# Windowed attention and two feed-forward stages on one core: a fixed step for the attention halves, and new addresses for the split operands

## The chip, the cores and the metric

The kernel runs on one core of one Trainium2 chip. The time is device microseconds (us) of one execution, the median of three runs. The profile is of one further execution, taken by the hardware profiler.

## What is computed

Queries, keys and values of 4 batches, 8 heads, 576 positions and width 64 go through attention in which a position sees itself and the 63 before it. The result, 2304 tokens by 512, passes two feed-forward stages:

```python
scores = scale * np.matmul(q, k.transpose(0, 1, 3, 2))
mask = (rel >= 0) & (rel < window)            # window = 64
attn = softmax(np.where(mask, scores, -1e9))
x = np.matmul(attn, v)                        # then 2304 x 512
a = x @ w1                                    # 512 x 1024
b = x @ w2
x = (a * b @ w3) @ w_out                      # 1024 x 1024, 1024 x 512
h = x @ w_in                                  # 512 x 2048
out = (h * sigmoid(h)) @ w_out2               # 2048 x 512
```

## The kernel before

**Stages.** Weights first (0 to 88.9 us of the trace): they come as 64-bit floats, are unpacked on ScalarE, VectorE and GpSimd, and `w3 @ w_out` is formed on TensorE. Then phase A, nine blocks (`blk` 0 to 8) of 256 tokens: per block 192 products on line 718 (tiles `ab`: a and b, 16 steps `s` of 12 products) and 96 on line 743 (tile `x`). Then the stage for `h` (line 1028) and the output stage (line 1179), from 476.8 us to the end.

**Products.** Every operand is kept as a rounded ("high") part and the rest ("low"), both fp32r. One product of matrices is three passes (`PASSES`): high by high, high weight by low data, low weight by high data. The data are the moving operand, 256 columns in phase A and in the output stage. `split` makes the parts: a CAST on ScalarE (line 117) for the high one, a subtraction on GpSimd or VectorE (line 120) for the low one. The tiles are `xa`, `xb` (tokens into phase A) and `p` (a times b); within a tile the high part began 544 and 2096 elements of 4 bytes into it, the low part 0 and 16. 544 elements are 2176 bytes, 8 x 256 + 128; 2080 are 8320, 32 x 256 + 128: the two parts began 128 bytes apart within a stretch of 256. In the output stage all high and low moving operands begin at one offset within 256 bytes.

**Attention.** 74 groups `g` of two heads and a window of queries; 14 run in the weight stage, 60 within phase A. A group has two halves. `half(2g)` (even) issues on TensorE the scores of group g (tile `s`, lines 399 to 407), the values of group g-2 (tile `o`, lines 483, 484) and the transposes of group g-1 (tile `t`, line 450); on VectorE it issues the row maximum (line 414) and the splits of the transposes (lines 463, 465), on ScalarE their CASTs (460, 462) and the exponentials (line 428). `half(2g+1)` (odd) has the normalisation on VectorE (lines 436, 438, 440), which the transposes of the next even half wait for, the sum of the values (491 to 495), and the splits and loads of a later group. Some groups (`plain`) come split already and have fewer steps. All engines run their instructions in the order of the program.

**What sets the order.** `unit(n)` stands ahead of every 12 products (24 units a block). It calls `halves_to`, which runs halves up to number 28 + (24 blk + n + 1) * 5 // 7: 5 halves in 7 units. Halves thus stand 12 or 24 products apart, even ones mostly 36 and sometimes 24. Attention ends with block 6; blocks 7 and 8 have products alone.

**`w_in`.** 16 pieces of `w_in` are converted during phase A: a load on SyncE's queue (line 149, into `xe`), `scale` and `rest` on ScalarE (224, 229), `fraction`, `sign(0)`, `sign(1)` on VectorE (232, 236) with an addition on GpSimd (241) behind the last, and a store (244). `between` holds these steps by unit; `squeeze` runs those that are due in a unit, in an even half and after an evacuation. Loads and stores hang on `moves`.

**Blocks 7 and 8.** The operands of the next stage (`x_raw`, `x_sum`, `x_op`; loads of line 988) are made by `hooks_x` in block 7 from its unit 0 on, and parts of `w_in` are loaded (`r_load`, line 852) in unit 19 of block 7 and unit 0 of block 8.

## Time and profile before

| | us |
|---|---|
| Median of three runs | 827.35 (826.8 to 829.11) |
| Profiled execution, its own time | 829.54 |
| Its span in the trace | 827.8 |
| TensorE busy | 806.9 (97%) |
| VectorE, ScalarE, GpSimd busy | 633.0, 554.1, 339.4 |
| Weight stage | 88.9 |
| Phase A, blocks 0 to 6 | 320.0 |
| Phase A, blocks 7 and 8 | 67.9 |
| Stage for `h` and output stage | 351.0 |

The profile gives for each engine the time in which one of its instructions ran, and for each idle stretch what ended it. A matmul is busy from its start to its end, and the next one starts before that end: a busy TensorE can still run at different spacings. "Mean ns" of a matmul is the length of one, not the spacing.

### The profile page before, as it was taken

To read this page: it belongs to the slowest core of one execution; us is meant where nothing else is said; L and a number is where in the kernel's file an instruction comes from. 1 tells how busy PE (TensorE), PEld (TensorE's weight loads), DVE (VectorE), ACT (ScalarE), POOL (GpSimd) and SP (SyncE) were. 2 spreads that over 40 slices of the span, in tenths; PEclk is the share of its full clock that TensorE was granted. 3 is DMA by queue.
4 is the path that set the end of the run, shared out by engine and by line. 5 is a ranking of instruction groups with operands and counts; after the bars stand their busy time and mean duration, and the time that the engine had idled before them with its cause. 6 is when DMAs were issued, how large, how long until landed. Compare 5 with 4: busy or idle time off the path is not lost.

```text
span 827.8 us, 17223 instructions
## 1 busy us (share of the span) xinstructions
PE 806.9 (97%) x5930; PEld 762.2 (92%) x5930; DVE 633.0 (76%) x1537; ACT 554.1 (67%) x1278; POOL 339.4 (41%) x404
## 2 busy tenths in 40 slices
PE   8999999999998999999999999999999999999998
PEld 3455799899998999999999999999999999999998
DVE  7888858888888887898561669765654899998782
ACT  6899768888888887888541567765656664443340
POOL 5678656676866776777422402444100000000000
PEclk9999999999999999999999999999999999999999
DMA  9998243444543555454313128999567755554421
GB/s 309 336 315 284 74 157 101 135 150 151 176 151 114 159 164 166 135 160 128 115 52 102 64 97 301 314 300 371 206 245 251 238 165 157 165 156 131 151 77 51
DMA packets 81526, 146.44 MB, mean 177 GB/s; under 512 B 7072, under 2 KB 47904, under 8 KB 81440
## 3 DMA queue, kind: packets, MB, share of 16 engines
q1 hardware_dynamic: 76384, 140.47, 51.9%
q10 hardware_dynamic: 5056, 4.88, 1.8%
q8 instruction: 47, 0.77, 0.4%
q14 instruction: 39, 0.32, 0.1%
HBM read 105.48 MB, written 39.85 MB: 176 GB/s over the span
## 4 chain that ended last, share of the span: by engine, by line
PE 60%; ACT 10%; DVE 9%; issue 6%; POOL 3%; DMA 2%; SPq 0%; ACTq 0%; DVEq 0%; POOLq 0%
PE ab L718 12%; PE oa L1179 10%; PE ob L1179 8%; PE x L743 7%; PE ha L1028 6%; PE hd L1028 6%; PE hb L1028 6%; PE hc L1028 3%; ACT sm L428 2%; DVE a L726 1%; POOL klo L373 1%; ACT qkhi L367 1%; DVE sm L414 1%; PE t L450 1%; DVE sm L440 1%
## 5 line engine op out<-in xcount | busy, mean ns | idle before, releaser
L718 PE MATMUL ab<-xa,hl 128*128 128x256 f32 x864 | 128.2, 284 | 0.1
L718 PE MATMUL ab<-xb,hl 128*128 128x256 f32 x864 | 125.2, 280 | 0.0
L718 PEld LDWEIGHTS ab<-xa,hl 128*128 128x128 f32 x864 | 111.4, 188 | 0.9 <-DVE wp L120 0.9
L718 PEld LDWEIGHTS ab<-xb,hl 128*128 128x128 f32 x864 | 111.9, 188 | 0.0
L743 PE MATMUL x<-p,wp 128*128 128x256 f32 x864 | 109.1, 285 | 0.0
L743 PEld LDWEIGHTS x<-p,wp 128*128 128x128 f32 x864 | 105.0, 191 | 0.0
L1179 PE MATMUL oa<-wo_w,hi 128*128 128x256 f32 x408 | 73.7, 276 | 0.0
L373 POOL TENSOR_TENSOR klo<-qk,qkhi 64x192 fp32r<-64x192 f32 x110 | 70.6, 642 | 7.2 <-ACT qkhi L367 3.1
L120 POOL TENSOR_TENSOR p<-a,p 128x512 fp32r<-128x512 f32 x36 | 48.7, 1354 | 47.5 <-ACT p L117 47.5
L1179 PEld LDWEIGHTS oa<-wo_w,hi 128*128 128x128 f32 x408 | 61.4, 188 | 0.0
L1179 PE MATMUL oa<-wo_w,lo 128*128 128x256 f32 x204 | 56.3, 276 | 0.0
L117 ACT CAST p<-a 128x512 fp32r<-128x512 f32 x36 | 22.4, 621 | 49.0 <-DVE a L726 49.0
L1028 PE MATMUL ha<-xop,wi_w 128*128 128x384 f32 x288 | 53.9, 336 | 0.0
L428 ACT ACTIVATE sm<-sm,nm 128x192 f32<-128x192 f32 x110 | 49.3, 449 | 5.5 <-DVE nm L414 3.9
L1028 PEld LDWEIGHTS ha<-xop,wi_w 128*128 128x128 f32 x288 | 50.1, 188 | 0.1
L495 POOL TENSOR_TENSOR xr<-ot 128x128 f32<-128x128 f32 x43 | 25.4, 590 | 55.1 <-DVE ot L494 42.5
L1028 PE MATMUL hd<-xop,wi_w 128*128 128x384 f32 x252 | 47.6, 336 | 0.0
L414 DVE CUSTOM_DVE_ANT_0 sm<-s,consts 128x192 f32<-128x192 f32 x144 | 45.5, 353 | 2.3 <-PE s L407 1.1
L726 DVE TENSOR_TENSOR a<-ab,a 128x512 f32<-128x512 f32 x36 | 24.9, 691 | 29.2 <-PE ab L718 28.5
L367 ACT CAST qkhi<-qk 128x768 fp32r<-128x768 f32 x55 | 45.9, 834 | 1.2
L896 POOL TENSOR_TENSOR cv_b<-cv_b,cv_r 128x512 int32<-128x512 int32 x16 | 22.8, 1422 | 58.3 <-ACT wi_w L880 28.4
L450 PE MATMUL t<-consts,sm 128*128 128x128 f32 x216 | 35.9, 275 | 10.6 <-DVE sm L440 6.8
(276 smaller groups left out, 2190.9 us busy)
## 6 DMA issues: line engine op xcount, KB each, us to landing
qk<-in_qkv SPq DMA_DIRECT2D x55, 384.0 KB, 3.1
gd<-gxa SPq DMA_DIRECT2D x24, 384.0 KB, 5.0
words<-in_w SPq DMA_DIRECT2D x16, 512.0 KB, 6.6
xe<-in_w_in SPq DMA_DIRECT2D x16, 512.0 KB, 5.1
gq<-in_w_out SPq DMA_DIRECT2D x16, 512.0 KB, 5.6
words<-in_w3t SPq DMA_DIRECT2D x15, 512.0 KB, 6.7
gd<-gst SPq DMA_DIRECT2D x18, 384.0 KB, 5.1
xe<-gd SPq DMA_DIRECT2D x13, 512.0 KB, 4.1
```

The source lines that it names most:

```text
L120: (nc.vector if eng_lo == "dve" else nc.gpsimd).tensor_tensor(out=lo, in0=src, in1=f32(hi), op=ALU.subtract)
L367: nc.scalar.copy(out=hi, in_=t)
L373: nc.gpsimd.tensor_tensor(out=k_lo[g % 2][hs, h * 192 : h * 192 + 192], in0=t[hs, n], in1=f32(hi[hs, n]), op=ALU.subtract)
L414: nc.vector.tensor_tensor_reduce(out=sm[g % 2][:, h, :], in0=s_ps[:, h, :], in1=consts[:, at + 64 - 64 * h : at + 256 - 64 * h], op0=ALU.a ...
L428: nc.scalar.activation(out=e[:, h, :], in_=x, func=AF.Exp, scale=-1.0, bias=nm[:, h : h + 1], accum_out=sums_of[g % 2][:, h, 0:1])
L450: nc.tensor.transpose(t_ps[:, i * 128 : i * 128 + 128], x[:, at : at + 128], id_sb)
L495: nc.gpsimd.tensor_tensor(out=to, in0=t[:, 0:128], in1=t[:, 128:256], op=ALU.add)
L718: nc.tensor.matmul(acc[:, j * NA : j * NA + NA], lhsT=w[:, l, fs], rhs=x[k // 2][r][:, k % 2], start=(j == 0 and k == 0 and n == 0), stop= ...
L726: nc.vector.tensor_tensor(out=a_sb[:, 1], in0=acc, in1=a_sb[:, 0], op=ALU.mult)
L743: nc.tensor.matmul(acc[:, o * NA : o * NA + NA], lhsT=wp[f][:, l, at : at + 128], rhs=p[r][:, f], start=(n == 0), stop=((o, f) not in [y[: ...
L1028: nc.tensor.matmul(bank[name][:, q, 0:NB], lhsT=w[:, l, first + kt], rhs=x[:, kt, r, :], start=(fresh and kt == 0 and n == 0), stop=(kt == ...
L1179: nc.tensor.matmul(dst, lhsT=lhs[l], rhs=rhs[r], start=(first and e == 0 and q == 0 and n == 0), stop=(e == DUOS - 1 and q == 1 and n == 2 ...
```

## The change

Four things change; no instruction is added or removed on any engine. **(1)** In `xa` and `xb` the parts now begin at elements 32 and 544, in `p` at 48 and 2096: 2048 bytes (8 x 256) and 8192 bytes (32 x 256) apart, one offset within 256 bytes. **(2)** `tick`, ahead of every product, runs a half every 18 products, so that an even half stands every 36, at the same eight places in each block (products 6, 42, ... 258); the last half falls at product 132 of block 7. **(3)** The passes of `w_in` are keyed by the even half (`between`, one pass on VectorE in each of three groups in a row) and by the product (`moves`: load 104 products ahead, `scale` 39, `rest` 3, store 117 after). Two calls of `squeeze` in the evacuations go. **(4)** `hooks_x` runs from unit 13 of block 7 to unit 12 of block 8; `r_load` 0 and 1 move to unit 2 of block 8, 3 and 4 to its unit 7.

```diff
--- before.py
+++ after.py
@@ -247,18 +247,17 @@
 
     weights = {}
     line = []
-    between, unit_of = {}, [0]
+    between = {}
 
     moves = {}
 
-    def events(u):
-        if u in moves:
-            moves[u]()
-
-    def squeeze(u):
-        for k in sorted(k for k in between if k <= u):
-            for f in between.pop(k):
-                f()
+    def events(n):
+        for f in moves.pop(n, ()):
+            f()
+
+    def squeeze(g):
+        for f in between.pop(g, ()):
+            f()
     done = {"load": 0, "step": 0}
 
     def loads_to(n):
@@ -504,7 +503,7 @@
         if not odd:
             if g < NG:
                 scores(g)
-            squeeze(unit_of[0])
+            squeeze(g)
 
             def rest():
                 if 2 <= g <= NG + 1:
@@ -549,7 +548,7 @@
 
     def split_x(blk, part):
         t = slot(f"{'xa' if part == 0 else 'xb'}{blk}", "xa" if part == 0 else "xb", [1056], F32R)
-        x = [t[:, i : i + 512].rearrange("p (c n) -> p c n", c=2) for i in (544, 0)]
+        x = [t[:, i : i + 512].rearrange("p (c n) -> p c n", c=2) for i in (32, 544)]
         xhl.setdefault(blk, {})[part] = x
         split(x[0], x[1], column(4 * blk + 2 * part, 2), "act", "pool")
 
@@ -695,15 +694,15 @@
     def phase_a(blk, hooks):
         x = xhl[blk]
         t = slot(f"p{blk}", "p", [4160], F32R, skip=0)
-        p = [t[:, i : i + 8 * NA].rearrange("p (f n) -> p f n", f=8) for i in (2096, 16)]
+        p = [t[:, i : i + 8 * NA].rearrange("p (f n) -> p f n", f=8) for i in (48, 2096)]
 
         def unit(n):
-            u = 24 * blk + n
-            squeeze(u - 2)
-            unit_of[0] = u
-            halves_to(W_HALVES + (u + 1) * 5 // 7)
-            events(u)
             hooks(n)
+
+        def tick(n):
+            n += 288 * blk
+            halves_to(W_HALVES + (n + 12) // 18)
+            events(n)
 
         for s in range(16):
             i, m, j = s // 4, s // 2 % 2, s % 2
@@ -715,6 +714,7 @@
             for k in range(4):
                 w = weights["12", (2 * m + f // 4) * 4 + k]
                 for n, (l, r) in enumerate(PASSES):
+                    tick(12 * s + 3 * k + n)
                     nc.tensor.matmul(
                         acc[:, j * NA : j * NA + NA], lhsT=w[:, l, fs], rhs=x[k // 2][r][:, k % 2],
                         start=(j == 0 and k == 0 and n == 0), stop=(k == 3 and n == 2), skip_group_check=True,
@@ -724,8 +724,6 @@
                 nc.scalar.copy(out=a_sb[:, 0], in_=acc)
             elif j:
                 nc.vector.tensor_tensor(out=a_sb[:, 1], in0=acc, in1=a_sb[:, 0], op=ALU.mult)
-                if i < 3:
-                    squeeze(unit_of[0])
                 hi, lo = [y[:, 2 * i : 2 * i + 2] for y in p]
                 split(hi, lo, a_sb[:, 1].rearrange("p (f n) -> p f n", f=2), "act", "pool")
         for i in range(2):
@@ -739,12 +737,12 @@
                     unit(16 + 4 * i + n // 12)
                     if blk + 1 < NBLK and i == 0 and n in (12, 36):
                         split_x(blk + 1, n // 36)
+                tick(192 + 48 * i + n)
                 at = (2 * i + o) * 128
                 nc.tensor.matmul(
                     acc[:, o * NA : o * NA + NA], lhsT=wp[f][:, l, at : at + 128], rhs=p[r][:, f],
                     start=(n == 0), stop=((o, f) not in [y[:2] for y in todo[n + 1 :]]), skip_group_check=True,
                 )
-            squeeze(unit_of[0])
             x2 = slot(f"x2s{blk}_{i}", "st", [2, NA], bufs=4)
             nc.scalar.copy(out=x2, in_=acc.rearrange("p (o n) -> p o n", o=2))
             nc.scalar.dma_start(
@@ -768,16 +766,18 @@
         xe = slot("xe", "xe", [2304])
         phase_w()
         new_pt()
-        W_IN = 14
+        W_IN = 21
         for i in range(16):
             qq, k = divmod(i, 4)
             cols = slice(qq * 512, (qq + 1) * 512)
             c = Stored(None, w_in[k * 128 : (k + 1) * 128, cols], xe[:, i % 2 * 1024 : i % 2 * 1024 + 1024], w_in32[k, :, cols])
             load, *pieces, store = c.pieces()
-            for at, f in zip((2, 5, 6, 9, 12), pieces):
-                between.setdefault(W_IN + 9 * i + at, []).append(f)
-            moves[W_IN + (9 * i - 3 if i > 1 else 2 * i - 6)] = load
-            moves[W_IN + 9 * i + 16] = store
+            g = W_IN + 3 * i
+            at = 6 + 36 * (g - W_HALVES // 2)
+            for x, f in ((-104, load), (-39, pieces[0]), (-3, pieces[1]), (117, store)):
+                moves.setdefault(at + x, []).append(f)
+            for x in range(3):
+                between[g + x] = [pieces[2 + x]]
 
         def hooks0(n):
             steps_to(W12_B + 24 + (n + 1) * (20 - W12_B) // 7, (nc.vector, nc.gpsimd))
@@ -785,11 +785,15 @@
         phase_a(0, hooks0)
         for blk in range(1, NBLK - 2):
             phase_a(blk, lambda n: None)
-        late.close()
-
-        end = ctx.enter_context(tc.tile_pool(name="end", bufs=1, side="right"))
-        for i in (6, 0, 2, 3, 5, 4, 1):
-            slot(f"first_x{i}", f"x{i}", [1], pool=end)
+        end = None
+
+        def open_end():
+            nonlocal end
+            late.close()
+            end = ctx.enter_context(tc.tile_pool(name="end", bufs=1, side="right"))
+            for i in (6, 0, 2, 3, 5, 4, 1):
+                slot(f"first_x{i}", f"x{i}", [1], pool=end)
+
         PAIRS = FF2 // 256
         SUPER = T // (2 * NB)
         DUOS = PAIRS // 2
@@ -1233,18 +1237,25 @@
         def hooks_x(n):
             run_later()
             if n == 0:
+                open_end()
                 tmp["t1"] = xe[:, 1536:2304].rearrange("p (k n) -> p k n", k=2)
                 x_raw(0)
             if n in X5:
                 X5[n][0](*X5[n][1:])
-            if n == 19:
+
+        def hooks4(n):
+            if n >= 13:
+                hooks_x(n - 13)
+
+        def hooks5(n):
+            hooks_x(n + 11)
+            if n == 0:
+                r_load(2, slot("r2", "xr", [1024]))
+            if n == 2:
                 t = slot("r01", "q", [2048])
                 r_load(0, t)
                 r_load(1, t[:, 1024:2048])
-
-        def hooks5(n):
-            if n == 0:
-                r_load(2, slot("r2", "xr", [1024]))
+            if n == 7:
                 r_load(3, xe)
                 r_load(4, xe[:, 1024:2048])
             if n == 20:
@@ -1284,7 +1295,7 @@
         for k, f, m in ((26, f_load, 2), (26, f_sums, 1), (27, f_high, 1)):
             at(FIRST_OUT + k, f, m)
 
-        phase_a(NBLK - 2, hooks_x)
+        phase_a(NBLK - 2, hooks4)
         phase_a(NBLK - 1, hooks5)
         mid.close()
         pso = ctx.enter_context(tc.tile_pool(name="pso", bufs=1, space=PSUM, reuse_waits="tile"))
```

TensorE in block 3, from the products of tile `x` on (line 743 before, 742 after; a row ends in the number of equal instructions). Before, from one group's transposes to the next group's scores:

```order
527 L450 MATMUL t_3737<-consts,sm_77 128x128 x3
528 L743 MATMUL x_3_0_3721<-p_3239,wp_619 128x256 x3
529 L743 MATMUL x_3_0_3721<-p_3239,wp_623 128x256 x3
530 L743 MATMUL x_3_0_3721<-p_3239,wp_654 128x256 x3
531 L743 MATMUL x_3_0_3721<-p_3239,wp_658 128x256 x3
532 L743 MATMUL x_3_0_3721<-p_3239,wp_1021 128x256 x3
533 L743 MATMUL x_3_0_3721<-p_3239,wp_1025 128x256 x3
534 L743 MATMUL x_3_0_3721<-p_3239,wp_619 128x256 x3
535 L743 MATMUL x_3_0_3721<-p_3239,wp_623 128x256 x3
536 L403 MATMUL s_3797<-qkhi_3681 128x192 x2
537 L407 MATMUL s_3797<-klo_79,qkhi_3681 128x384
```

After, from the products behind the transposes of the corresponding group on:

```order
517 L718 MATMUL ab_14_3582<-xb_3028,hl 128x256 x6
518 L742 MATMUL x_3_0_3656<-p_3166,wp_619 128x256 x3
519 L742 MATMUL x_3_0_3656<-p_3166,wp_623 128x256 x3
520 L742 MATMUL x_3_0_3656<-p_3166,wp_654 128x256 x3
521 L742 MATMUL x_3_0_3656<-p_3166,wp_658 128x256 x3
522 L742 MATMUL x_3_0_3656<-p_3166,wp_1021 128x256 x3
523 L742 MATMUL x_3_0_3656<-p_3166,wp_1025 128x256 x3
524 L742 MATMUL x_3_0_3656<-p_3166,wp_619 128x256 x3
525 L742 MATMUL x_3_0_3656<-p_3166,wp_623 128x256 x3
526 L742 MATMUL x_3_0_3656<-p_3166,wp_654 128x256 x3
527 L742 MATMUL x_3_0_3656<-p_3166,wp_658 128x256 x3
528 L402 MATMUL s_3713<-qkhi_3592 128x192 x2
```

Between two groups stood 24 products there; now 36 (the 6 of the first row and ten rows of 3).

VectorE at the same place. Before, the multiplication of a by b (L726, it reads tile `ab`) and a pass of `w_in` (L236, `cv_b`) stand ahead of the row maximum (L414, printed as ISA):

```order
599 L379 TENSOR_TENSOR qkhi_3681<-qk_3523,qkhi_3681 64x256
600 L726 TENSOR_TENSOR a_3_3670<-ab_14_3693,a_3_3670 128x512
601 L236 SCALAR_TENSOR_TENSOR cv_b<-xe,cv_b 128x256
602 L414 ISA sm_78,nm_3727<-s_3723,consts 128x192
603 L414 ISA nm_3727 128x1
604 L414 ISA sm_78,nm_3727<-s_3723,consts 128x192
605 L414 ISA nm_3727 128x1
606 L463 TENSOR_TENSOR pt_1038<-t_3737,pt_1038 128x2x128
607 L465 TENSOR_TENSOR pt_1036<-t_3737,pt_1036 64x64 x2
608 L436 TENSOR_REDUCE rs_3728<-es_87 128x2
609 L438 RECIPROCAL rs_3728<-rs_3728 128x2
610 L440 TENSOR_TENSOR sm_78<-sm_78,rs_3728 128x384
```

After:

```order
575 L378 TENSOR_TENSOR qkhi_3592<-qk_3419,qkhi_3592 64x256
576 L413 ISA sm_78,nm_3626<-s_3622,consts 128x192
577 L413 ISA nm_3626 128x1
578 L413 ISA sm_78,nm_3626<-s_3622,consts 128x192
579 L413 ISA nm_3626 128x1
580 L236 SCALAR_TENSOR_TENSOR cv_b<-xe,cv_b 128x256
581 L462 TENSOR_TENSOR pt_1038<-t_3635,pt_1038 128x2x128
582 L464 TENSOR_TENSOR pt_1036<-t_3635,pt_1036 64x64 x2
583 L726 TENSOR_TENSOR a_3_3580<-ab_14_3582,a_3_3580 128x512
584 L435 TENSOR_REDUCE rs_3627<-es_87 128x2
585 L437 RECIPROCAL rs_3627<-rs_3627 128x2
586 L439 TENSOR_TENSOR sm_78<-sm_78,rs_3627 128x384
```

The pass now follows the row maximum, and the multiplication stands right ahead of the normalisation (L435 to L439).

ScalarE there. Before, the cast of a times b (L117) and `scale` (L224, it reads the load in `xe`) are ahead of the casts of the transposes (L460, L462):

```order
419 L492 COPY ot_3675<-o_3642 64x256
420 L367 CAST qkhi_3681<-qk_3523 128x768
421 L388 CAST vhl_3683<-v_3436 128x3x64
422 L117 CAST p_3239<-a_3_3670 128x512
423 L224 ACTIVATE cv_b<-xe 128x512
424 L460 CAST pt_1038<-t_3737 128x2x128
425 L462 CAST pt_1036<-t_3737 64x64 x2
426 L428 ACTIVATE sm_78,es_87<-sm_78,nm_3727 128x192 x2
427 L491 COPY ot_3764<-o_3733 64x256
428 L492 COPY ot_3764<-o_3733 64x256
```

After:

```order
409 L427 ACTIVATE sm_78,es_87<-sm_78,nm_3626 128x192 x2
410 L117 CAST p_3166<-a_3_3580 128x512
411 L117 CAST xa_3669<-xr 128x512
412 L490 COPY ot_3675<-o_3631 64x256
413 L491 COPY ot_3675<-o_3631 64x256
414 L366 CAST qkhi_3681<-qk_3507 128x768
415 L387 CAST vhl_3683<-v_3421 128x3x64
416 L224 ACTIVATE cv_b<-xe 128x512
417 L459 CAST pt_1039<-t_3727 128x2x128
418 L461 CAST pt_1037<-t_3727 64x64 x2
419 L427 ACTIVATE sm_77,es_86<-sm_77,nm_3717 128x192 x2
```

The L224 of after belongs to the piece whose load stands 65 products ahead; before, 36 products lay between the load and this L224. It still stands right ahead of the casts of the transposes.

## Rows read from the trace of the kernel before

**Rows 1.** the page, part 1: busy us, share of the span, instructions
```profile
PE 806.9 (97%) x5930; PEld 762.2 (92%) x5930; DVE 633.0 (76%) x1537; ACT 554.1 (67%) x1278; POOL 339.4 (41%) x404
```
**Rows 2.** windows, blocks 0 to 6 and 8: stretch, length, busy (instructions) per engine, clock
```profile
88.90:138.70 49.80, 46.83 (x382) 45.15 (x383) 35.20 (x105) 37.12 (x102) 31.09 (x38) 1.00 0.37 115
138.70:185.40 46.70, 44.29 (x372) 43.64 (x370) 39.72 (x123) 39.78 (x115) 32.69 (x44) 1.00 0.45 141
185.40:229.10 43.70, 42.88 (x363) 42.67 (x361) 37.00 (x125) 36.93 (x110) 31.58 (x43) 1.00 0.49 158
229.10:275.90 46.80, 44.50 (x370) 43.72 (x369) 38.93 (x122) 38.76 (x113) 32.01 (x43) 1.00 0.43 132
275.90:322.40 46.50, 44.91 (x363) 44.31 (x362) 39.12 (x130) 38.23 (x113) 33.75 (x45) 0.96 0.52 163
322.40:366.20 43.80, 43.80 (x370) 43.59 (x369) 37.22 (x117) 38.17 (x110) 30.21 (x40) 1.00 0.52 160
366.20:408.90 42.70, 41.64 (x354) 41.46 (x353) 33.72 (x109) 32.33 (x97) 29.88 (x39) 1.00 0.35 110
...
442.90:476.80 33.90, 33.90 (x291) 33.90 (x290) 15.81 (x26) 14.44 (x27) 11.16 (x13) 1.00 0.20 64
```
**Rows 3.** windows of 30 us, from block 7 and from the output stage
```profile
410.00:440.00 30.00, 30.00 (x257) 30.00 (x256) 15.31 (x15) 11.71 (x18) 9.15 (x6) 1.00 0.21 72
690.00:720.00 30.00, 30.00 (x267) 30.00 (x266) 29.66 (x61) 14.46 (x24) 0.00 (x0) 1.00 0.54 165
```
**Rows 4.** lines by form, TensorE, 436.2 to 436.6 us, block 7: xcount | busy us, mean
```profile
L743 PE MATMUL x<-p,wp 128*128 128x256 f32 x5 | 0.8, 281 | 0.0
```
**Rows 5.** the page, part 5: the same columns, a line of the output stage
```profile
L1179 PE MATMUL oa<-wo_w,hi 128*128 128x256 f32 x408 | 73.7, 276 | 0.0
```
**Rows 6.** lines by form, TensorE, 401.9 to 402.3 us, in block 6
```profile
L743 PE MATMUL x<-p,wp 128*128 128x256 f32 x6 | 0.8, 277 | 0.0
```
**Rows 7.** waits of TensorE, blocks 0 to 6: us in total, times, longest
```profile
PE t L450 <- DVE sm L440: 5.6, 6, 1.3
PE t L450 <- ACT qkhi L367: 1.9, 2, 1.1
PE t L450 <- ACT vhl L388: 1.5, 1, 1.5
PE o L483 <- DVE pt L463: 1.5, 1, 1.5
```
**Rows 8.** timeline from 256 us, block 3: start, us, instruction [idle before <-releaser]
```profile
256.46 0.42 SPq L149 DMA_DIRECT2D xe<-in_w_in  x1
...
261.54 0.66 ACT L224 ACTIVATE cv_b<-xe 128x512 f32<-128x512 f32 x1 [0.74 <-DMA xe<-in_w_in]
...
262.83 0.42 DVE L463 TENSOR_TENSOR pt<-t,pt 128x256 fp32r<-128x256 f32 x1 [1.69 <-ACT pt L462]
...
263.40 0.47 PE L483 MATMUL o<-pt,vhl 128*128 128x256 f32 x2 [1.49 <-DVE pt L463]
...
264.23 0.56 DVE L440 TENSOR_TENSOR sm<-sm,rs 128x384 f32<-128x384 f32 x1
...
264.94 0.52 PE L450 MATMUL t<-consts,sm 128*128 128x128 f32 x3 [0.82 <-DVE sm L440]
```
**Rows 9.** windows, the stretch at the lower clock in block 4
```profile
318.30:321.70 3.40, 3.40 (x19) 3.40 (x18) 3.04 (x13) 1.64 (x7) 2.39 (x4) 0.50 0.12 23
```
**Rows 10.** timeline at 162 us, block 1, GpSimd and VectorE
```profile
162.45 1.29 POOL L241 TENSOR_TENSOR cv_b<-cv_b,cv_r 128x512 int32<-128x512 int32 x1 [1.16 <-DVE rs L436]
...
162.67 1.48 DVE L440 TENSOR_TENSOR sm<-sm,rs 128x384 f32<-128x384 f32 x1
```
**Rows 11.** the page, part 6: DMA issues, KB each, us to landing
```profile
xe<-in_w_in SPq DMA_DIRECT2D x16, 512.0 KB, 5.1
```
**Rows 12.** DMA issues between 400 and 480 us, the same columns
```profile
r<-w_in SPq DMA_DIRECT2D x3, 512.0 KB, 3.7
...
xe<-x2d SPq DMA_DIRECT2D x1, 768.0 KB, 6.2
```

## The prediction

> **What bounds the kernel now.** I read the page first, then windows by block, then TensorE's waits, and last the timeline around one wait. The page says that TensorE is busy 97% of the span [rows 1], so only two things can give time: its idle stretches, and the spacing of its products. By blocks [rows 2], a block without attention (block 8) takes 33.9 us for 288 products, 117.7 ns each. Block 5, with attention and without a moment of idle TensorE, takes 43.8: 9.9 us more for its share of the groups. Five halves in 7 units are 8.57 groups a block, so a group costs 9.9 / 8.57 = 1.16 us of TensorE when nothing is late. Blocks 0, 1, 3 and 4 take 46.5 to 49.8. Length minus busy time over blocks 0 to 6 is 3.0 + 2.4 + 0.8 + 2.3 + 1.6 + 0 + 1.1 = 11.2 us. The waits name it [rows 7]: ten stops, almost all transposes that wait for the normalisation or for ScalarE. Each stop costs a little more than its idle: a matmul is busy for 0.28 us [rows 4], its successor would have started 0.118 after it, so 0.16 is lost ahead of the idle. 11.2 + 10 x 0.16 = **12.8 us** is what waits cost.
>
> Why they are late: per group VectorE works 37.22 / 8.57 = 4.3 us and ScalarE 38.17 / 8.57 = 4.5 us in block 5, 4.6 us each in block 1 [rows 2]. A step of 24 products lasts 24 x 0.1177 + 1.16 = 4.0 us, one of 36 lasts 5.4. In a short step both engines fall behind, and the next transposes wait. Rows 8 show one case at its worst: the load of a `w_in` piece is issued at 256.46, ScalarE's `scale` stands idle for it 0.74 us until 261.54, the casts of the transposes are queued behind `scale`, so VectorE's split starts only at 262.83 after 1.69 us idle, the values wait 1.49 us, and the transposes behind them another 0.82.
>
> The second thing is the spacing. Products of the same shape, 256 columns, run in the output stage too. In 30 us the trace counts 257 matmuls in block 7 and 267 in the output stage [rows 3]; some 2.4 of each count only overlap the edges, so the spacings are 30 / 254.6 = 117.8 and 30 / 264.6 = **113.4 ns**. A matmul's own length shows the same two values: 281 ns in block 7 and 276 here [rows 4, 5]. The clock is 1.00 in both, and VectorE is busier in the faster stretch (29.66 of 30 us against 15.31), so it is not that other engines disturb phase A. What differs is the address: phase A alternates between high and low data 128 bytes apart within 256, the output stage stays at one offset.
>
> **Part 1, the addresses.** The edit gives phase A what the output stage has. Bounds: nothing, or 2592 x 4.3 = 11.1 us (all products at 113.4). For it speaks rows 3; one more sign is in block 6, where a short row of eight products that read high data only runs at 277 ns [rows 6]. Against it: the same eight stand in each block, and in block 7 they run at 281 [rows 4], as in all other blocks but one; one address is not all, the quick state has to be entered. In phase A it is broken every 36 products by a group of other shapes. I take 115 ns for the 2148 products up to the last half and 113.7 for the 444 behind it: 2148 x 2.7 + 444 x 4.0 ns = 5.8 + 1.8 = **7.6 us** gained.
> The trace does not say why addresses should matter. The Trainium skill, page "SBUF — State Buffer", section "Who interferes with whom", speaks against it: TensorE has a read port of its own for the moving operand and another for weights, and waits for nobody; by that rule this part gives nothing. Rows 3 show two spacings for one shape and one clock, which the rule does not foresee, but no run here has moved an address alone.
>
> **Part 2, a half every 18 products.** The work is the same, 60 groups x 1.16 us. Every step is now 36 x 0.115 + 1.16 = 5.3 us against 4.3 to 4.6 us of work on VectorE and ScalarE, so each keeps some 0.7 us of slack in every cycle, where it had -0.5 in the short ones. At two places of a block (products 96 and 192) the multiplication of a by b stands right ahead of a normalisation, and eats into that slack. Of the 12.8 us I leave 1.5: block 0 converts the last weights as well, and its normalisations are now queued behind such steps on VectorE. Gain **11.3 us**; bounds 6 (half the stops move to new places) and 12.8. GpSimd's share stays 30 to 34 us of a block [rows 2]; its results are needed several us later, so it is priced at nothing; if that cover went, its 1.3 us addition would show once per piece.
> The stretch at the half clock goes with the stops: at 318.30 to 321.70 the granted clock is 0.50 (1.2 GHz) [rows 9], right behind the longest stop, and 19 matmuls ran where 3.4 / 0.118 = 29 and the edges' 2 would have: 12 x 0.118 = 1.4, with the pause before it some **1.6 us**. The cause that I see is the stop in block 4; without it I expect 1.00 throughout.
>
> **Part 3, `w_in`'s passes.** The load now stands 65 products and two groups ahead of `scale`, 65 x 0.115 + 2 x 1.16 = 9.8 us, where the case of rows 8 had 36 and one, 5.4. A load lands 5.1 us after its issue [rows 11]; SyncE may issue it up to 4.7 us late, behind attention's loads, and `scale` still doesn't wait. That removes the worst stop and is counted in part 2. On VectorE one pass stands behind the row maximum of each even half, no longer two in a step. GpSimd's addition follows `sign(1)` in every third group. The stores move on SyncE's queue past a pair of attention loads, which have two groups of time: nothing.
>
> **Part 4, blocks 7 and 8.** VectorE, ScalarE and GpSimd are busy 15 to 16, 14 and 11 of 34 us there [rows 2, 3]. 3.7 groups enter block 7 (some 17 us of work each on VectorE and ScalarE), the operands slide by 13 units (18 us): 31 + 17 = 48 of 68 us. Loads of operands take 6.2 us to land and of `w_in` 3.7 [rows 12]; `r_load` 0 stands 6 units (72 products, 8.3 us) ahead of its first use, so at least 2 us are spare. Nothing, at worst one late load: 2 us. The stages behind are untouched.
>
> **Sum.** 7.6 + 11.3 + 1.6 = 20.5 us. The profiled execution took 829.54, 1.7 more than its span and 2.2 more than the median of runs; 829.54 - 20.5 = 809.0 for such an execution, and 827.35 - 20.5 = 806.9 for the median. I say **807**.
>
> **The rivals.**
> *The addresses do nothing.* The spacing stays 117.7, the 12.9 us of parts 2 and 3 remain: 814.4. For it: seven of nine short rows; and the groups that break the row every 36 products. Chance 0.17. The rule of the Trainium skill cited above would give this time.
> *The waits come back at fixed places.* 36 divides 288, so each block repeats the same eight places; one late place is late some seven times. If most of the 12.8 us returns and the clock falls again, only the addresses remain: 827.35 - 7.6 = 819.7. Against it is the slack of 0.7 us. Chance 0.12.
> *Slower, through VectorE against GpSimd.* The normalisation's multiplication takes 0.56 us [rows 8], but 1.48 where GpSimd's addition for `w_in` had begun 0.22 us earlier [rows 10]: 0.92 more, above the 0.7 us of slack if nothing was gained ahead. The new order fixes which GpSimd work meets which normalisation. If 0.92 is lost in 30 of the 60 groups, it is 27.6 us against 20.5: 834.5. It decides the sign from 22 groups on. Against it: the addition comes in 16 groups only, the rest would have to come from GpSimd's other subtractions, and VectorE's busy time of rows 2 holds such meetings already. Chance 0.06.
> The Trainium skill states the mechanism (page "SBUF — State Buffer", section "Who interferes with whom"): a VectorE instruction with two inputs in SBUF contends with a GpSimd instruction that reads SBUF. Rows 10 agree, 1.48 against 0.56.
> *Nothing adds up:* the stops move, the spacing stays, within 2.5 us of before: chance 0.04. *Below 801*, from gains that no row shows: 0.03.
>
> **How the numbers follow.** The likeliest case, both parts as worked out, has 0.58, between 801.9 (all at 113.4, no stop left: 25.5 us) and 812 (half of either missing). A range of 800 to 818 takes this, the case without addresses, and the half of the returning waits: 0.58 + 0.17 + 0.06 + 0.02 = 0.83. 0.3%, 2.5 us, is about what a measurement of this kernel can tell from no change. Faster by more: 0.58 + 0.17 + 0.12 + 0.03 = 0.90; within: 0.04; slower: 0.06.
>
> **What would show it.** The addresses: 266 or 267 matmuls in 30 us of block 8, and 276 ns in the line of `ab`, not 281. The step: blocks 1 to 6 all near 288 x 0.115 + 8 x 1.16 = 42.4 us, block 7 near 33.1 + 3.7 x 1.16 = 37.4, TensorE's waits in phase A under 2 us, no stretch below clock 1.00. `scale` never waits for its load. Wrong would be: equal stops in every block at one place, a line `ab` at 280 or above, or `h` products (line 1028) that wait for `w_in`'s parts.

## The result, and the profile after

The changed kernel takes **816.0 us** (median of 4 runs, 815.52 to 816.56) against 828.23 of the kernel before beside it: ratio 0.985, 95% interval 0.983 to 0.987. It is faster by 12 us, inside the forecast range, 9 us above the forecast of 807. A second set of runs gave 816.24. The profiled execution has a span of 814.8 us, 13.0 less than before.

| stretch | before, us | after, us | difference |
|---|---|---|---|
| weight stage | 88.9 | 87.7 | -1.2 |
| phase A | 387.9 | 373.7 | -14.2 |
| stages for `h` and output | 351.0 | 353.4 | +2.4 |

The 1.2 us of the weight stage are not the change's: its instructions are the same in both kernels, and a second trace of the changed kernel has 88.5 there.

The page of the changed kernel, part 1; it answers to [rows 1]:

```profile
PE 799.4 (98%) x5930; PEld 755.4 (93%) x5930; DVE 637.8 (78%) x1537; ACT 555.7 (68%) x1278; POOL 337.2 (41%) x404
```

Its windows by block (blocks 1 to 3, 7 and 8), then 30 us of block 8; columns as in [rows 2, 3]:

```profile
133.20:175.80 42.60, 42.08 (x362) 41.90 (x361) 36.77 (x117) 36.82 (x106) 30.12 (x41) 1.00 0.49 156
175.80:218.70 42.90, 42.23 (x363) 42.03 (x362) 37.71 (x117) 37.12 (x107) 30.63 (x41) 1.00 0.50 157
218.70:262.00 43.30, 42.18 (x363) 41.76 (x362) 36.86 (x116) 36.70 (x107) 31.02 (x41) 1.00 0.47 144
...
390.70:427.50 36.80, 36.80 (x317) 36.80 (x316) 21.63 (x46) 17.30 (x44) 14.38 (x16) 1.00 0.26 82
427.50:461.40 33.90, 33.90 (x290) 33.90 (x289) 20.09 (x31) 17.41 (x31) 11.07 (x12) 1.00 0.33 110
...
430.00:460.00 30.00, 30.00 (x257) 30.00 (x256) 18.77 (x28) 15.43 (x28) 10.26 (x12) 1.00 0.34 114
```

Blocks 1 to 6 now take 42.6 to 43.3 us, where four of seven took 46.5 or more. The clock is 1.00 in all of them; the stretch of [rows 9] is gone. But block 8 takes 33.9 us as before, and its 30 us hold 257 matmuls, not 266: there the new addresses did nothing. Block 7 takes 36.8, and no engine makes TensorE idle in it.

TensorE's waits in phase A of the changed kernel; they answer to [rows 7]:

```profile
PE t L449 <- DVE sm L439: 6.1, 8, 1.3
```

One kind is left, the transposes that wait for the normalisation. Two of the eight stops are in block 0, the other six all at one place, product 258 of blocks 1 to 6. The timeline of the changed kernel around that place in block 2, and around two stretches of products in block 2 (starts and lengths in us, idle time and its releaser in brackets):

```profile
180.35 0.84 PE L718 MATMUL ab<-xb,hl 128*128 128x256 f32 x6
181.03 0.84 PE L718 MATMUL ab<-xa,hl 128*128 128x256 f32 x6
...
183.49 0.87 PE L718 MATMUL ab<-xa,hl 128*128 128x256 f32 x6
184.20 0.87 PE L718 MATMUL ab<-xb,hl 128*128 128x256 f32 x6
...
209.09 1.28 POOL L120 TENSOR_TENSOR xa<-xr,xa 128x512 fp32r<-128x512 f32 x1
...
209.31 1.35 DVE L378 TENSOR_TENSOR qkhi<-qk,qkhi 64x256 fp32r<-64x256 f32 x1
...
212.92 1.29 POOL L120 TENSOR_TENSOR xb<-xq,xb 128x512 fp32r<-128x512 f32 x1
...
212.94 1.68 DVE L439 TENSOR_TENSOR sm<-sm,rs 128x384 f32<-128x384 f32 x1
...
214.77 0.52 PE L449 MATMUL t<-consts,sm 128*128 128x128 f32 x3 [0.68 <-DVE sm L439]
```

Two things are to be seen. First the spacing: six products that last 0.84 us from the first start to the last end are 113.3 ns apart (5 x 0.1133 + 0.276), six that last 0.87 are 117.8 apart. A group lies between the two pairs of rows. From the starts of all products: the stretch of 35 products between two groups runs from end to end at the one or at the other spacing, and through blocks 1 to 6 (29 stretches at 113.3, 19 at 117.8) the two take turns, group by group, behind 36 of the 38 groups in which TensorE wasn't held up; behind the ten others mostly not. Second the place at 258: VectorE's multiplication (L439) began 0.02 us after GpSimd's subtraction for `xb` and took 1.68 us, its own 0.56 and nearly all of the 1.29 of the other. In the same step, L378 met the subtraction for `xa` and took 1.35 in place of 0.42.

Behind phase A, two stops are new: 0.52 us at 653.3 for a conversion on VectorE, and 1.45 us at 533.78, for a copy on ScalarE that stood behind a conversion that waited for a load of `w_out`. The timeline at the longer one:

```profile
532.38 0.67 ACT L224 ACTIVATE cv_b<-gq 128x512 f32<-128x512 f32 x1 [2.30 <-DMA gq<-in_w_out]
...
533.78 0.97 PE L1032 MATMUL ha<-xop,wi_w 128*128 128x384 f32 x4 [1.45 <-ACT gxa L1054]
```

### The profile page after: what moved, and what is told of

It is laid out like the page before. It is cut to its first block, busy times and chain, and to the rows that moved or that the text cites. A ratio compares the mean times of both kernels' runs of the same rounds, so it can differ in the third digit from the quotient of the medians.

```text
span 814.8 us, 17206 instructions
## 1 busy us (share of the span) xinstructions
PE 799.4 (98%) x5930; PEld 755.4 (93%) x5930; DVE 637.8 (78%) x1537; ACT 555.7 (68%) x1278; POOL 337.2 (41%) x404
## 4 chain that ended last, share of the span: by engine, by line
PE 73%; DVE 8%; ACT 3%; issue 2%; DMA 2%; SPq 0%; ACTq 0%; DVEq 0%
PE ab L718 21%; PE oa L1183 10%; PE ob L1183 8%; PE x L742 7%; PE ha L1032 6%; PE hd L1032 6%; PE hb L1032 5%; PE hc L1032 3%; PE t L449 2%; DVE sm L439 1%; PE o L482 1%; DMA gst<-t 1%; PE s L402 1%; PE s L406 1%; DVE qkhi L378 1%
## 5 line engine op out<-in xcount | busy, mean ns | idle before, releaser
L718 PE MATMUL ab<-xb,hl 128*128 128x256 f32 x864 | 127.4, 283 | 0.0
L718 PE MATMUL ab<-xa,hl 128*128 128x256 f32 x864 | 123.3, 279 | 0.1
L742 PE MATMUL x<-p,wp 128*128 128x256 f32 x864 | 104.6, 280 | 0.0
L742 PEld LDWEIGHTS x<-p,wp 128*128 128x128 f32 x864 | 101.4, 188 | 0.0
L117 ACT CAST p<-a 128x512 fp32r<-128x512 f32 x36 | 22.3, 621 | 41.1 <-DVE a L726 41.1
L439 DVE TENSOR_TENSOR sm<-sm,rs 128x384 f32<-128x384 f32 x55 | 46.3, 842 | 1.9
L494 POOL TENSOR_TENSOR xr<-ot 128x128 f32<-128x128 f32 x43 | 25.3, 589 | 46.5 <-DVE ot L493 38.8
L1032 PEld LDWEIGHTS hd<-xop,wi_w 128*128 128x128 f32 x252 | 44.0, 188 | 0.0
```

The lines of the kernel that those rows point to most:

```text
L439: nc.vector.tensor_tensor(out=x, in0=e, in1=rs.unsqueeze(2).to_broadcast([128, 2, 192]), op=ALU.mult)
L494: nc.gpsimd.tensor_tensor(out=to, in0=t[:, 0:128], in1=t[:, 128:256], op=ALU.add)
L718: nc.tensor.matmul(acc[:, j * NA : j * NA + NA], lhsT=w[:, l, fs], rhs=x[k // 2][r][:, k % 2], start=(j == 0 and k == 0 and n == 0), stop= ...
L742: nc.tensor.matmul(acc[:, o * NA : o * NA + NA], lhsT=wp[f][:, l, at : at + 128], rhs=p[r][:, f], start=(n == 0), stop=((o, f) not in [y[: ...
L1032: nc.tensor.matmul(bank[name][:, q, 0:NB], lhsT=w[:, l, first + kt], rhs=x[:, kt, r, :], start=(fresh and kt == 0 and n == 0), stop=(kt == ...
```

## The experiments

**Theory after the result:** the step of 18 carries the gain; the addresses save some 5 us of products, since a stretch runs fast only in one of two states; the six stops at 258 come from GpSimd's instructions that hold up VectorE's. Rivals: the addresses do nothing, or what they do is eaten by waits; VectorE is simply full at 258; the new places of `w_in`'s passes are what counts.

### The addresses: taken out, and alone

In the changed kernel:

```diff
-        x = [t[:, i : i + 512].rearrange("p (c n) -> p c n", c=2) for i in (32, 544)]
+        x = [t[:, i : i + 512].rearrange("p (c n) -> p c n", c=2) for i in (544, 0)]
-        p = [t[:, i : i + 8 * NA].rearrange("p (f n) -> p f n", f=8) for i in (48, 2096)]
+        p = [t[:, i : i + 8 * NA].rearrange("p (f n) -> p f n", f=8) for i in (2096, 16)]
```

> The changed kernel with the parts of the split operands back at the old offsets (a high and a low part 128 bytes apart within 256). Theory: the new addresses let a stretch of products run at 113.3 ns between two groups, but only about every second stretch of blocks 1 to 6 does, block 8 none, so they are worth 5.4 us: 816.0 goes to about 821.4, and no stretch of phase A stays at 113.3 ns. Rival 1, the addresses do nothing and what shortened the products is the new place of the groups: 816 as it was, stretches at 113.3 as before. Rival 2, as forecast, 7.6 us: 823.6. The stops of TensorE at product 258 of a block should stay in all cases, 0.7 to 1.4 us each.

Measured: 818.46 us (818.41 to 819.32), ratio to before 0.987 (0.984 to 0.990). The products went back to 117.6 ns on average (115.5 in the changed kernel, over all that don't come first behind a group), 2530 x 2.1 = 5.3 us. The time rose by 2.2 to 2.5 only. TensorE's waits in phase A tell why; this is their row:

```profile
PE t L449 <- DVE sm L439: 4.0, 7, 1.1
```

4.0 us of stops with products 117.6 ns apart, 6.1 with 115.5: with the new addresses 2.1 of the 5.3 us are given back in waits, 1.8 of them at 258, where the shorter step meets the same chain on VectorE. So both the theory (5.4 us of products) and its rival (waits eat it) were half of the truth. Only these two sets of addresses were run: that it is the offset within 256 bytes that counts, and nothing else in which they differ, is not shown.

The same edit the other way round, in the kernel before:

> The kernel before with the new offsets of the split operands and nothing else. Theory: the same gain as in the changed kernel where groups stand 24 or 36 apart, 4 to 6 us of 828, with stretches at 113.3 and at 117.8 ns between groups, and blocks 7 and 8 wholly at the one or the other. Rival 1 (the addresses do nothing without the new places of the groups): within 1 us of the kernel before. Rival 2 (waits eat the gain, since VectorE and ScalarE get less time between two groups): the products are shorter, TensorE's waits longer by the same, and the time within 2 us of before.

Measured: 827.75 (10 runs) against 828.78, ratio 0.9987 (0.9973 to 1.0002): rival 2. The products were shorter there too (114.4 to 115.6 ns in blocks 0 to 6, 117.8 in all of blocks 7 and 8), 4.9 us in all. The time shows about 1 of them. TensorE's waits rose from 11.0 to 13.7 us, which is over half of what is missing; the rest is not accounted for. Two of the rows, which stood at 5.6 and 1.5 before [rows 7]:

```profile
PE t L450 <- DVE sm L440: 7.6, 9, 1.3
...
PE t L450 <- ACT vhl L388: 1.9, 2, 1.5
```

### The passes of `w_in`: back to their old places

```diff
-            g = W_IN + 3 * i
-            at = 6 + 36 * (g - W_HALVES // 2)
-            for x, f in ((-104, load), (-39, pieces[0]), (-3, pieces[1]), (117, store)):
-                moves.setdefault(at + x, []).append(f)
-            for x in range(3):
-                between[g + x] = [pieces[2 + x]]
+            for at, f in zip((2, 5, 6, 9, 12), pieces):
+                between.setdefault(W_IN + 9 * i + at, []).append(f)
+            moves[W_IN + (9 * i - 3 if i > 1 else 2 * i - 6)] = load
+            moves[W_IN + 9 * i + 16] = store
```

with `W_IN = 14`, `squeeze` and `events` by units as before.

> The changed kernel with the conversion of w_in in its old places (steps by units of 12 products, run in units, even halves and evacuations, loads and stores by units), and all else as changed. This takes part 3 of the change alone. Theory: the steady step of 36 products is what removed most stops, but the old passes bunch on VectorE and the loads come 36 to 60 products ahead, so stops return at changing places: waits of 8.0 us rise to 11 to 14, the time to 818.5 to 821. Rival 1: the passes' places are worth nothing, 816 within 1. Rival 2: they carry most of what the waits lost (6.8 us): 822 or more.

Measured: **812.73** (812.13 to 814.85), ratio 0.983 (0.980 to 0.985), 3.3 us faster than the changed kernel. No theory had this: the new places cost time. Its waits in phase A, and its timeline at the same product 258 of block 2:

```profile
PE t L450 <- DVE sm L440: 3.9, 7, 1.3
```

```profile
212.74 0.56 DVE L440 TENSOR_TENSOR sm<-sm,rs 128x384 f32<-128x384 f32 x1
...
212.83 1.62 POOL L120 TENSOR_TENSOR xb<-xq,xb 128x512 fp32r<-128x512 f32 x1
```

Here VectorE was first, by 0.09 us; it takes 0.56, TensorE has no stop, and GpSimd pays (1.62 for 1.29). In the changed kernel GpSimd was first by 0.02. So a few hundredths decide whether the multiplication takes a microsecond more. Whether TensorE stops for it is another matter, as block 4 of the same kernel shows at 258:

```profile
297.10 1.29 POOL L120 TENSOR_TENSOR xb<-xq,xb 128x512 fp32r<-128x512 f32 x1
297.11 1.70 DVE L440 TENSOR_TENSOR sm<-sm,rs 128x384 f32<-128x384 f32 x1
...
298.95 0.52 PE L450 MATMUL t<-consts,sm 128*128 128x128 f32 x3
```

GpSimd was first and the multiplication took 1.70, yet TensorE has no stop: the multiplication began 4.1 us after the scores of the group ahead, at 222, in place of 4.9 in block 4 of the changed kernel, and ended before TensorE got to the transposes. With the old places GpSimd is first at 258 in five of blocks 1 to 6 (not in block 2), and the multiplication begins 0.1 to 0.8 us sooner in each; one normalisation earlier VectorE is ahead by as much already (0.5 us in block 1, 0.8 in block 4), and where it gains this is not followed here. Blocks 1, 2 and 4 have no stop there; blocks 3, 5 and 6 keep 0.6 to 0.7. Of the 55 normalisations in blocks 0 to 6 that don't come split, 14 take over a microsecond here, 16 in the changed kernel and 15 in the kernel before: the meetings are much the same, and what the old places give is time ahead of the deadline at 258.

### The step alone

The two undoings together leave the half every 18 products and the later operands of blocks 7 and 8, which were not run apart.

> The changed kernel with the old addresses and the old places of w_in's passes: what is left of the change is the half every 18 products and the later operands in blocks 7 and 8. Theory, from sums of single undoings (816.0 + 2.5 for the addresses - 3.3 for the passes): 815.2 within 1, so the step alone carries nearly all of the gain; waits in phase A 3 to 5 us, spacing 117.7 throughout. Rival 1, the new passes are needed with old addresses too: 819 or more. Rival 2, a slower product hides more of the stops, and with old addresses the passes' place is worth nothing: 818 to 819.

Measured: 816.33 (815.78 to 816.77), ratio 0.985 (0.984 to 0.987). The products stand at 117.6 ns, the clock at 1.00, and this is all that TensorE waits for in phase A:

```profile
PE t L450 <- DVE sm L440: 1.8, 3, 1.1
```

The sum of the single undoings had given 815.2, with waits of 3 to 5 us. So the four corners are, in us (time; length of phase A in the trace; TensorE's waits in it):

| | old places of the passes | new places |
|---|---|---|
| old addresses | 816.33; 374.4; 1.8 | 818.46; 376.5; 4.0 |
| new addresses | 812.73; 372.0; 3.9 | 816.0 and 816.24; 373.8 and 373.9; 6.1 and 5.9 |

The step alone brings 12.0 us, as much as the whole change. By the times, the new addresses save 2.2 to 3.6 us and the new places of the passes cost 2.1 to 3.5. Each time is from four executions, which spread by up to 3.7 us, and the kernel before took 828.2 to 828.8 beside them, so these differences are good to about 1 us. Phase A alone is clearer: there the addresses save 2.4 to 2.7 and the new places cost 1.8 to 2.1, much the same in either row and column, and either of the two adds 1.9 to 2.2 us of waits. The rest lies outside phase A, where the instructions are the same.

The changed kernel ran once more beside it:

> The changed kernel itself, beside the next three. Theory: 816 within 1. In its first profile TensorE stopped 1.4 us in the stage for h for a load of w_out that landed late; if that belongs to the program it comes again, if it is chance the part behind phase A shrinks from 349.8 to 348 us and the stop is gone.

816.24 (814.39 to 818.1). The stop at the load of `w_out` was gone, yet the part behind phase A still took 352.3 us, with a stop of 0.9 for another load's conversion. In the other kernels run here that part took 351.2 to 353.0. The kernel with the old addresses had the stop too (1.5 us). Its instructions are the same in all; how its loads fall is not settled here.

### What holds the normalisation up

> The changed kernel, but the low parts of xa and xb of blocks 1 to 8 (16 subtractions of 128x512) are made on VectorE instead of GpSimd. In the changed kernel TensorE stops at product 258 of blocks 1 to 6 for 0.7 to 1.4 us, and there the normalisation's multiplication takes 1.7 us instead of 0.56 while GpSimd runs. Theory: VectorE is held up by GpSimd's instructions that read SBUF, at this place the two subtractions for xa and xb; with them on VectorE the multiplication takes 0.56 there, the six stops of about 1 us (with 0.16 each) shrink to under 0.3, and the time falls by 3 to 6 us to 810 to 813. Rival 1: VectorE is simply overloaded at this place; 0.7 to 1 us more of work twice there makes the stops longer, 818 to 822. Rival 2: the stops are due to the addition for w_in alone, which meets this place in two of six blocks; four stops stay and the time is 815 to 817.

```diff
-        split(x[0], x[1], column(4 * blk + 2 * part, 2), "act", "pool")
+        split(x[0], x[1], column(4 * blk + 2 * part, 2), "act", "dve" if blk else "pool")
```

Measured: 825.12 (824.08 to 827.28), ratio 0.995 (0.994 to 0.997): slower than the changed kernel by 9 us. Its timeline ahead of product 222 of block 2:

```profile
209.43 0.61 ACT L117 CAST xa<-xr 128x512 fp32r<-128x512 f32 x1
...
210.08 1.56 DVE L120 TENSOR_TENSOR xa<-xr,xa 128x512 fp32r<-128x512 f32 x1 [1.21 <-ACT xa L117]
...
211.94 0.56 DVE L439 TENSOR_TENSOR sm<-sm,rs 128x384 f32<-128x384 f32 x1
...
212.64 0.52 PE L449 MATMUL t<-consts,sm 128*128 128x128 f32 x3 [1.44 <-DVE sm L439]
```

The multiplication takes 0.56 here and at 258 (1.26 there in blocks 3 and 6, where it meets the addition for `w_in`), as the theory had it, and five of six stops at 258 are gone. But the subtraction now stands ahead of the normalisation in VectorE's order and waits 1.21 us for a cast that ScalarE has behind other work, so the stop moved to product 222 and grew (1.0 to 2.4 us, in blocks 0 to 6). Behind the last of them, in block 6, the granted clock was 0.50 (from 389.7 to 393.0 us). The time that the theory gave (810 to 813) was missed by far for this reason. Not rival 1 either: VectorE was idle, not full.

> The changed kernel, but the normalisation of the groups of phase A that don't come split multiplies each head by its column with one instruction that reads a single tensor (two of 128x192) instead of one instruction with two tensors (128x384, 0.56 us undisturbed, 1.7 us at product 258). Theory: the instruction with two tensors in SBUF is held up by GpSimd, the one with a single tensor isn't; the two take about 0.3 us each everywhere, the six stops at product 258 (6.1 us of wait) fall to under 1.5, and the time from 816 to 810 to 812. Rival 1: any VectorE instruction is held up by GpSimd there, so the two together take 1.5 us or more and the time stays at 816 within 1. Rival 2: the place is late since its exponentials are late, whatever the multiplication takes: at least 4 of the 6.1 us stay, 814 to 816.

```diff
-        nc.vector.tensor_tensor(out=x, in0=e, in1=rs.unsqueeze(2).to_broadcast([128, 2, 192]), op=ALU.mult)
+        if g < 14 or plain(g):
+            nc.vector.tensor_tensor(out=x, in0=e, in1=rs.unsqueeze(2).to_broadcast([128, 2, 192]), op=ALU.mult)
+            return
+        for h in range(2):
+            nc.vector.tensor_scalar(out=x[:, h], in0=e[:, h], scalar1=rs[:, h : h + 1], scalar2=None, op0=ALU.mult)
```

Measured: 815.81 (814.4 to 817.7), no difference in the median. With the granted clock at 1.00 throughout it took 814.4 and 814.5, with a fall of it 817.1 and 817.7. Rival 1: the instruction with a single tensor is held up as well. Its timeline at 258 of block 3:

```profile
256.77 1.27 POOL L241 TENSOR_TENSOR cv_b<-cv_b,cv_r 128x512 int32<-128x512 int32 x1
256.80 2.60 DVE L443 TENSOR_SCALAR sm<-sm,rs 128x192 f32<-128x192 f32 x2
...
258.00 1.28 POOL L120 TENSOR_TENSOR xb<-xr,xb 128x512 fp32r<-128x512 f32 x1
258.31 0.30 PE L453 MATMUL t<-consts,sm 128*128 128x128 f32 x1 [0.82 <-DVE sm L443]
...
259.45 0.44 PE L453 MATMUL t<-consts,sm 128*128 128x128 f32 x2 [0.85 <-DVE sm L443]
```

Two instructions can be caught twice: each waited out one of GpSimd's, and TensorE stopped twice, here and in block 6. In blocks 1, 2, 4 and 5, where GpSimd has only the subtraction at this place, the first of the two was caught and the stops at 258 fell from 0.5 to 0.7 us to 0.2 or nothing.

Its windows at the same place of block 6 show what can come behind such a stop, as [rows 9] did in block 4 before: the granted clock is down to 0.73 on average right behind it. It doesn't come each time: behind the same double stop in block 3 the clock stayed at 1.00, and in the changed kernel behind stops of 1.12 us too.

```profile
386.00:390.00 4.00, 2.32 (x14) 2.07 (x14) 3.92 (x10) 2.83 (x8) 2.91 (x4) 0.84 0.50 177
390.00:394.00 4.00, 4.00 (x28) 4.00 (x28) 2.82 (x10) 2.79 (x9) 2.46 (x6) 0.73 0.34 96
```

### What sets the spacing of a stretch

In a group of the changed kernel TensorE runs scores, values, transposes. Three kernels change that order (for groups of phase A that don't come split), as here, where the transposes go ahead of the values. The other two leave the last group with transposes, in block 7, as it was.

```diff
             def rest():
+                late_t = 1 <= g <= NG and (g < 14 or plain(g))
+                if 1 <= g <= NG and not late_t:
+                    split_t(g - 1, transposes(g - 1))
                 if 2 <= g <= NG + 1:
                     sums.append(values(g - 2))
                     if plain(g - 2):
                         sums.pop()()
-                if 1 <= g <= NG:
+                if late_t:
                     split_t(g - 1, transposes(g - 1))
```

> The changed kernel with the transposes of a group ahead of its values on TensorE (for groups of phase A that do not come split already): a group now ends with products of 256 columns instead of transposes of 128. In the changed kernel the stretches behind the groups of blocks 1 to 6 alternate between 113.3 and 117.8 ns. Theory: which spacing a stretch has is set by how the group ahead of it ends, so the alternation turns into one spacing for most stretches; if that is 113.3, the products gain up to 5 us more, if 117.8 they lose 5. Rival: the alternation has nothing to do with the end of the group and stays. In all cases the transposes are needed 0.35 us earlier, which can lengthen the stops at product 258 by that, 2 us in all.

Measured: 818.17 (two executions). The alternation was gone: every stretch from block 1 on ran at 117.8, up to the last group, which has values only; behind it block 8 ran at 113.3 from end to end. Its timeline across a group of block 4, and its 30 us in block 8:

```profile
269.05 0.87 PE L721 MATMUL ab<-xb,hl 128*128 128x256 f32 x6
...
271.43 0.28 PE L483 MATMUL o<-pt,vhl 128*128 128x256 f32 x1
271.55 0.87 PE L721 MATMUL ab<-xb,hl 128*128 128x256 f32 x6
```

```profile
433.00:463.00 30.00, 30.00 (x267) 30.00 (x267) 18.84 (x28) 16.08 (x29) 9.99 (x12) 1.00 0.36 118
```

> The changed kernel with the order values, transposes, scores on TensorE in a group (it is scores, values, transposes there; with scores, transposes, values nearly all stretches ran at 117.8 ns). Theory: the order alone sets a rule for the spacing behind a group: kept, turned over, or always the same one. Always 113.3 would take 3 to 4 us more off the products, of which the stops at product 258 may take half back: 813 to 815; always 117.8: 817 to 819; turned over each time: 816. Rival: the state is chance, not rule: stretches of both kinds in no pattern over blocks that have no stop. Which of the three rules it is, I can't tell beforehand.

Measured: 821.4. No single rule: stretches of both spacings follow each other in no pattern, 31 of 48 in blocks 1 to 6 at 117.8. Its waits took 7.3 us, and the time lies above all that the expectation had.

> The changed kernel with the order values, scores, transposes on TensorE in a group. Theory: what ends the group decides; it ends with transposes as in the changed kernel, so the stretches alternate between 113.3 and 117.8 ns as there, and the time is 816 within 1.5. Rival: the whole length of the group decides, not its end, and then this order too alternates, but so would have the one with the transposes ahead of the values, which did not; so an own rule of this order speaks for neither.

Measured: 814.38 (two executions, 813.68 and 815.09). The group ends with transposes as in the changed kernel, yet nearly all stretches of blocks 1 to 6 ran at 113.3 (44 of 48, against 29). The four stretches at 117.8 came behind groups with a stop or a short hold, at 258 and at 186, but four other stops at 258 were followed by fast ones. So not the end of a group decides, and which rule an order has I could only try. Its timeline across a group of block 2, the same place as in the changed kernel above:

```profile
180.55 0.84 PE L724 MATMUL ab<-xa,hl 128*128 128x256 f32 x6
181.23 0.40 PE L482 MATMUL o<-pt,vhl 128*128 128x256 f32 x2
...
181.99 0.49 PE L449 MATMUL t<-consts,sm 128*128 128x128 f32 x3
182.23 0.94 PE L724 MATMUL ab<-xb,hl 128*128 128x256 f32 x6
183.01 0.84 PE L724 MATMUL ab<-xa,hl 128*128 128x256 f32 x6
```

### A version that beats both

> The changed kernel with the old places of w_in's passes and, in a group, values ahead of scores and transposes. With the new passes this order left nearly all stretches of blocks 1 to 6 at 113.3 ns and the time at 814.4; the old passes with the old order gave 812.7. Theory: both add up: 812.7 - 1.5 = 811, stretches at 113.3 in blocks 1 to 6, block 8 at 117.8. Rival: the faster products meet the same VectorE, the stops grow by what the products gain: 812.7 within 0.5.

Measured: 813.05 (811.83 to 814.05), ratio 0.981 (0.979 to 0.983). Phase A was 1.5 us shorter than with the old order (370.5 against 372.0 us from its first to its last product), as the theory had it, but the part behind it 1.5 longer, with a stop of 1.1 for a load, and the weight stage 1.6; the time shows nothing of the gain.

> The previous kernel with one more turn: in the last group that has transposes (product 78 of block 7) they come ahead of the values. In all kernels but the one with transposes first, block 8 ran at 117.8 ns from end to end; there it ran at 113.3. Theory: the short last group of values alone turns the state over, a group with transposes first leaves the slow one; so with this order the stretch from 78 to 114 is slow, and all behind product 114 of block 7 is fast: 444 products x 4.4 ns = 2.0 less 0.2, about 1.8 us under the previous kernel, some 809. Rival: the state of block 8 is set by block 7's other work, not by its last groups: no difference, block 8 at 117.8.

Measured: **811.25** (809.68 to 811.53), ratio 0.979 (0.977 to 0.981): 1.8 us under the previous kernel, as expected, and 4.8 under the changed one. Block 8 runs fast. In block 3, though, six stretches in a row (products 43 to 257) ran at 117.8 in this order without a stop, so values ahead of scores and transposes don't always lead to a fast stretch. 30 us of block 8:

```profile
426.00:456.00 30.00, 30.00 (x267) 30.00 (x267) 18.84 (x28) 16.08 (x29) 9.99 (x12) 1.00 0.36 117
```

## Why the prediction came out as it did

The direction and the range were right; the gain came out 9 us smaller than forecast, and 816.0 lies inside the range only since that reached up to 818, drawn to take in the case without the addresses. In the profiled executions the gain is 13.0 us, 7.5 short of 20.5. Of these, 2.3 are products that gained less, 4.6 stops that stayed (6.1 us, where 1.5 was forecast) and 2.4 the part behind phase A, less 1.2 in the weight stage: 8.1, so the account closes to 0.6 us. Two of the signs that the prediction named for being wrong were there: stops in each of blocks 1 to 6 at one place, and a line `ab` above 280 ns (283 for the products of `xb`, 279 for those of `xa`). By its steps:

- **What bounds the kernel:** right. TensorE's idle time and the spacing were the two things that moved. The waits were the short steps' doing: with the step of 36 alone they fell from 11 to 1.8 us. One reading was off: the 43.8 us of block 5 hold nine groups, not 8.57, so a group costs 1.10 us and not 1.16; the sum of 20.5 doesn't use it.
- **Part 1, the addresses, 7.6 us:** the products gained 5.3. The failed step was "I take 115 ns for the 2148 products ... and 113.7 for the 444 behind": the first half held (115.0 in blocks 0 to 6), but I took the fast spacing for a state that a run of equal offsets finds by itself within a few products. It is one of two states that both held as long as nothing interrupted, and block 8 stayed in the slow one for all its 288 products. The rival "the addresses do nothing", with its 814.4, came close to the time, but for another reason. The rule of the Trainium skill set against this part (page "SBUF — State Buffer", section "Who interferes with whom": TensorE never waits on anyone) doesn't cover it: moving the addresses alone took the mean from 117.6 to 115.5 ns, at the same clock.
- **Part 2, the step, 11.3 us and 1.6 of clock:** 12.0 for the step alone, against 12.9 forecast with the clock's part. This term was right (with part 4, which the run includes), and the clock stays at 1.00 there and in the changed kernel.
- **Part 3, the passes, priced at nothing beyond that:** wrong in sign. They cost 2.1 us with the old addresses and 3.3 to 3.5 with the new, 1.8 to 2.1 of it in phase A. The failed sentence is "On VectorE one pass stands behind the row maximum ..., no longer two in a step", which counted work per step and not when the normalisation begins: with the new places its multiplication ahead of product 258 starts 0.1 to 0.8 us later, and what GpSimd adds to it then falls past the moment at which TensorE asks for it. The stop of [rows 8] by the late load doesn't come back with the old places either; the step of 36 had already covered it.
- **Faster products lengthen the waits.** I priced the addresses and the waits apart. With either places of the passes, the new addresses add some 2.1 us of waits (from 1.8 to 3.9, from 4.0 to 6.1), mostly at product 258, and the new places add as much with either addresses. The prediction said that the step keeps 0.7 us of slack, and had in its rival the 0.92 us that a meeting costs; the second is larger than the first, and at one place per block two such meetings follow each other. That rival had the mechanism, but a meeting alone costs TensorE nothing: 16 normalisations met GpSimd for so long, and only the six at 258 stopped it, where 30 of 60 were assumed; "back at fixed places" had the pattern.
- **Part 4, blocks 7 and 8:** right, no stop there.
- **Not foreseen:** the part behind phase A took 2.4 us longer in the profiled execution, though its instructions are the same, of which 1.45 is the late load shown above and 0.52 the other new stop. Whether a shorter phase A makes its loads fall worse stays open.

## What to carry to other kernels

Spread side work so that every step between two deadlines is long enough for the slowest helper: that alone was worth the whole of this change. Where two engines hold each other up, look at who starts first, and at how long before the deadline, not at how busy they are: 0.1 us of order was worth 1.1 us of VectorE, and TensorE stopped for it only where the instruction had begun too late to take it. And before a gain in spacing is added to a gain in waits, ask what the shorter step does to the chain that the waits came from; here waits took back some 40%, and in the kernel before over half.

## What the runs showed of the hardware that I had not expected

- Products of 256 columns with their moving operands at one offset within 256 bytes run at 113.3 or at 117.8 ns, at clock 1.00, and stay at what they begin with until another shape or a stop comes (block 8: 288 products at 117.8 in the changed kernel, at 113.3 in two others with the same products). With high and low parts 128 bytes apart the mean was 117.5 to 117.8 in every block at that clock.
- The order of a group's nine matmuls decides what happens to that state: scores, values, transposes turned it over (36 of 38 groups without a hold in the changed kernel); scores, transposes, values left it slow; values, scores, transposes left it fast (100 of 102 in three kernels) and turned a slow one fast in 9 of 14. Why is open; no run looked below the starts of instructions.
- A VectorE instruction that meets GpSimd's waits for nearly the whole of it (1.68 us for 0.56 against a subtraction of 1.29), also when it reads only one tensor and a column (two of them, 2.60 us). The Trainium skill (page "SBUF — State Buffer", section "Who interferes with whom") has the two share ports under an exclusive lock, and says that the order of issue decides who blocks. The two orders of start, 0.02 and 0.09 us apart, agree as to who waits; VectorE lost 1.12 of the 1.27 us in which both ran, GpSimd 0.33 of 0.47, so not quite the whole.
